# A two-layer product with four of seven partial products summed in one PSUM bank, three additions a set, and another order at the stage change

## The chip, the cores and the metric

The kernel runs on one core of one Trainium2 chip. The metric is the device time of the program in microseconds; lower is better. The engines are named as the profile names them: PE (matrix products), PEld (its weight loads), DVE (vector engine), ACT (scalar engine), POOL, and SP, whose queue issues most DMAs.

## The reference, cut to what matters

```python
scores = scale * np.matmul(q, k.transpose(0, 1, 3, 2))      # 4 batches, 12 heads, 448 x 448
scores = cap * np.tanh(scores / cap)
attn = np.exp(scores - np.max(scores, axis=-1, keepdims=True))
attn = attn / (np.sum(attn, axis=-1, keepdims=True) + 1e-09)
x = np.matmul(attn, v)                                      # laid out as 1792 tokens x 768
h = x @ w_in                                                # 768 -> 2048
g = h * np.cos(h)
out = g @ w_out                                             # 2048 -> 768
```

The weights `w_in` and `w_out` arrive as 64-bit floats and are turned into 32-bit words on the chip.

## The kernel before, in words

Three stages follow each other. **Attention** takes the first part of the program. **The first layer** multiplies `x` by `w_in`. Every factor is split into a high part and a low remainder, and each product of two factors is three matmuls (high by high, low by high, high by low). The 2 x 2 block scheme with seven products instead of eight is used: a *set* `s` is one pair of row blocks of `w_in` (index `g`, 0 to 7) with one half of the tokens (`p`, 0 or 1); there are 16 sets, listed in `ORDER`. The seven products of a set are called by the factor on the token side: `11`, `21`, `22` are blocks of `x`, `t1` to `t4` are differences of blocks. One product is 3 (pieces of the inner dimension) x 3 (high and low) = 9 matmuls of 128 x 448, so a set is 63 matmuls and the layer is 112 products. **The second layer** multiplies `g` by `w_out`, 1152 matmuls of the same size, which is 128 times nine.

A set accumulates in four PSUM banks, held as two tiles of two banks each. A tile of even sets is called `pair`, of odd sets `acc`. In `last_part` the set is brought together in SBUF: ACT copies bank a (line L797), DVE makes three additions with it (L800), then the last three products go on into banks a, d and c, ACT copies a again (L803), and DVE makes two more additions (L810). A result goes to DRAM (`hidden`) by a DMA of ACT's queue (L812). The second layer reads it back from there.

The factors of sets with p = 1 are made by DVE (`mix`, L186, a difference of blocks in place), split by ACT (`high`, L198) and by DVE (`low`, L201). For sets 2 and 3 this happens while PE works; it is the list `work[1]` and `work[2]`. Sets 0 and 1 use the p = 0 factors, which attention has made. The weights of a row block are made from raw words: ACT takes the magnitude (L257), DVE runs four steps (`clamp` L272, `shift` L275, `tail_bits` L278, `sign_bit` L282), and `sums` then makes the block sums (L306 to L312) and splits them (L544 on ACT, L293 and L299 on DVE). The words `u` have two buffers. For eight of the row blocks of `w_out` the words are stored to DRAM (`words`) and fetched again at the stage change (`fetch`), when the space of the p = 0 factors is free.

Each engine runs its instructions in the written order. What stands between the additions is taken from a list, `left`, by `fill(room)`: it takes entries until their costs (in us, written beside each) have used up the room. The second layer needs, for each `q` of 64, the gated values: ACT `turns` (L932), DVE two steps and ACT a sine (`cosine`, L937 to L939), DVE a product and ACT its high part (`gate`, L943, L944), DVE the remainder (`low`, L948); and for the first eight `q` the split of a fetched block of `w_out` (L901 on ACT, L904 on DVE). `second` issues the 18 matmuls of one `q` (L971). At the very end `evacuate` adds the last banks (L1011) and stores them (L1014).

## Time and profile before

| what | us |
|---|---|
| median of three runs | 652.08 |
| their range | 651.57 to 653.46 |
| the profiled execution's own time | 653.12 |
| its span, first to last instruction | 651.2 |
| PE busy in the span | 602.3 |
| DVE busy | 482.6 |
| ACT busy | 342.0 |

The busy time of PE is that of pipelined records, so it shows where PE stood still rather than how fast it was. DVE and ACT are busy for three quarters and half of the span. The granted clock of PE, over the whole span, is 0.971 of full speed.

### The profile page before, as it was taken

The page shows a single profiled execution, that of the slowest core. Times are in us where ns is not written, and L with a number is a line of the kernel's source. Part 1 is how long each engine was busy: PE and PEld are TensorE (multiplying, and loading weights), DVE is VectorE, ACT ScalarE, POOL GpSimd, SP SyncE. Part 2 cuts the span into 40 slices and gives each one's busy share as a digit, 9 for nine tenths or more (in the row PEclk, how much of TensorE's full clock was granted, in tenths as well). Part 3 has the DMA queues.
Part 4 walks back from the last instruction along what each step waited for, and adds up shares of the span by engine and source line. Part 5 has one row for each costly group of instructions (what it writes and reads, how often), then busy time and mean ns, then how long its engine had stood idle before and what let it go on. Part 6 is the DMA issues. An engine that isn't in the chain of part 4 may idle for free.

```text
span 651.2 us, 11970 instructions
## 1 busy us (share of the span) xinstructions
PE 602.3 (92%) x4962; PEld 467.9 (72%) x4962; DVE 482.6 (74%) x703; ACT 342.0 (53%) x479; POOL 13.0 (2%) x13
## 2 busy tenths in 40 slices
PE   9999999999837899999999788799999999999996
PEld 3333443346626799988989677699999999999985
DVE  3898999898495777777777664898796972577662
ACT  7999999991243322223222223676776662545340
POOL 0000012200000000000000000000000000000000
PEclk9999999999777999999999987899999999999999
DMA  8454334300212244364643768343333220514302
GB/s 286 141 176 128 117 120 132 110 20 2 106 56 97 106 153 153 130 199 134 233 159 125 240 225 302 106 144 123 105 109 131 85 71 0 172 69 156 115 14 88
DMA packets 39085, 83.66 MB, mean 128 GB/s; under 512 B 4339, under 2 KB 21747, under 8 KB 39027
## 3 DMA queue, kind: packets, MB, share of 16 engines
q1 hardware_dynamic: 34562, 68.86, 33.1%
q10 hardware_dynamic: 4464, 13.99, 5.3%
q8 instruction: 40, 0.66, 0.4%
q14 instruction: 19, 0.15, 0.1%
HBM read 59.51 MB, written 23.33 MB: 127 GB/s over the span
## 4 chain that ended last, share of the span: by engine, by line
PE 50%; DVE 25%; ACT 12%; DMA 8%; issue 4%; SPq 1%; ACTq 0%; DVEq 0%
PE acc L971 18%; PE pair L971 17%; DMA words<-u 5%; PE pair L409 4%; PE acc L489 4%; ACT t L428 4%; ACT t L424 4%; PE pair L730 4%; DVE sum L473 2%; PE acc L730 2%; DVE u L278 2%; DVE u L282 2%; DVE c L800 2%; ACT u L257 2%; DVE c L810 2%
## 5 line engine op out<-in xcount | busy, mean ns | idle before, releaser
L428 ACT ACTIVATE t<-t 128x1792 f32<-128x1792 f32 (+1 forms) x50 | 75.4, 1519 | 0.0
L489 PE MATMUL acc<-t,v 64*32 64x448 f32 x1344 | 73.8, 537 | 1.6 <-DVE x L527 1.5
L424 ACT ACTIVATE t<-pair 128x896 f32<-128x896 f32 x82 | 73.5, 966 | 2.9 <-PE pair L409 2.9
L409 PE MATMUL pair<-qk 64*32 64x448 f32 x1312 | 73.1, 542 | 0.3 <-ACT t L424 0.2
L489 PEld LDWEIGHTS acc<-t,v 64*32 64x32 f32 x1344 | 26.1, 107 | 39.5 <-issue 33.4
L409 PEld LDWEIGHTS pair<-qk 64*32 64x32 f32 x1312 | 25.0, 107 | 39.4 <-issue 20.7
L473 DVE TENSOR_TENSOR sum<-sum,t 128x1792 f32<-128x1792 f32 x25 | 50.5, 2019 | 0.5
L971 PE MATMUL pair<-g1h,wmixedh 128*128 128x448 f32 x96 | 30.7, 369 | 0.0
L272 DVE TENSOR_SCALAR u<-u 128x768 f32<-128x768 f32 x30 | 16.7, 556 | 16.3 <-ACT u L257 16.3
L971 PE MATMUL acc<-g1h,wmixedh 128*128 128x448 f32 x84 | 27.2, 369 | 0.0
L971 PE MATMUL acc<-g0h,wmixedh 128*128 128x448 f32 x84 | 26.6, 367 | 0.0
L939 ACT ACTIVATE f<-f 128x448 f32<-128x448 f32 x21 | 12.2, 581 | 25.8 <-DVE f L938 25.6
L939 ACT ACTIVATE f1l<-f1l 128x448 f32<-128x448 f32 x21 | 12.2, 580 | 23.9 <-DVE f1l L938 23.5
L257 ACT ACTIVATE u<-w 128x768 f32<-128x768 f32 x15 | 13.5, 900 | 21.2 <-DMA words<-u 14.7
L257 ACT ACTIVATE u<-raw 128x768 f32<-128x768 f32 x14 | 12.6, 899 | 21.7 <-DMA words<-u 13.7
L544 ACT CAST sums1h<-u 128x768 fp32r<-128x768 f32 (+1 forms) x16 | 11.7, 755 | 23.4 <-DVE u L308 13.1
L971 PE MATMUL pair<-g0h,wmixedh 128*128 128x448 f32 x72 | 23.1, 366 | 0.0
L939 ACT ACTIVATE f0l<-f0l 128x448 f32<-128x448 f32 x22 | 12.7, 579 | 17.8 <-DVE f0l L938 17.4
L971 PE MATMUL acc<-g0h,wownh 128*128 128x448 f32 x64 | 20.6, 367 | 1.4 <-ACT c L803 1.4
L971 PE MATMUL pair<-g0h,wownh 128*128 128x448 f32 x68 | 21.5, 366 | 0.0
L971 PE MATMUL pair<-g1h,wownh 128*128 128x448 f32 x52 | 17.6, 385 | 3.5 <-DVE g1h L948 2.7
L800 DVE TENSOR_TENSOR c<-c,pair 128x448 f32<-128x448 f32 x21 | 13.0, 621 | 10.0 <-ACT c L797 6.4
(405 smaller groups left out, 1628.7 us busy)
## 6 DMA issues: line engine op xcount, KB each, us to landing
hidden<-c ACTq DMA_DIRECT2D x28, 448.0 KB, 5.7
qk<-in_qk_dram SPq DMA_DIRECT2D x20, 448.0 KB, 3.9
w<-in_w_in_dram SPq DMA_DIRECT2D x18, 384.0 KB, 4.3
w<-in_w_out_dram SPq DMA_DIRECT2D x16, 384.0 KB, 3.5
raw<-in_w_out_dram SPq DMA_DIRECT2D x16, 384.0 KB, 3.6
v<-in_v_dram SPq DMA_DIRECT2D x42, 128.0 KB, 2.1
f0l<-hidden SPq DMA_DIRECT2D x22, 224.0 KB, 3.9
f<-hidden SPq DMA_DIRECT2D x21, 224.0 KB, 2.8
```

What stands on the lines that cost most here:

```text
L257: self.nc.scalar.activation(self.u[u].bitcast(F32), self.raw[k].bitcast(F32)[:, :, 1], AF.Abs, scale=F64_STEP)
L272: self.nc.vector.tensor_scalar(r, r, LEAST, MOST, op0=ALU.max, op1=ALU.min)
L278: self.nc.vector.scalar_tensor_tensor(self.u[u], self.raw[k][:, :, 0], 29, self.u[u], op0=ALU.logical_shift_right, op1=ALU.bitwise_or)
L409: self.nc.tensor.matmul(ps[o:o + 32, h, 0:S], lhsT=x[mine, k:k + 32], rhs=x[mine, Q], start=True, stop=True, tile_position=(64 * h, o))
L424: self.nc.scalar.activation(self.ts[i][:, k], self.ps.pop(j)[:, :, 0:S], AF.Tanh, scale=self.inv)
L428: self.nc.scalar.activation(t, t, AF.Exp, scale=self.capt)
L473: self.nc.vector.tensor_add(out, old, self.ts[NC * n + c])
L489: self.nc.tensor.matmul(self.acc[n, e][o, r], lhsT=self.v[n, c][rows, d], rhs=self.t(n, a, c)[rows, h], start=c == 0, stop=c == NC - 1, ti ...
L730: self.nc.tensor.matmul(out, lhsT=a, rhs=b, start=m < 4 and k == 0 and t == 0, stop=k == NQUAD - 1 and t == 2, skip_group_check=True)
L800: self.nc.vector.tensor_add(*adds[m])
L939: nc.scalar.activation(y, y, AF.Sin, scale=2.0 * math.pi)
L971: self.nc.tensor.matmul(self.out_bank(v, d)[:, 0:S], lhsT=w, rhs=x, start=v != 4 and j == 0 and i == 0, stop=v != 3 and j == HALF - 1 and ...
```

## The change: what it does

**In a set.** Four products (`11`, then `t2`, then `t3`, then `t4`) accumulate one after the other in bank 0, and after each ACT copies the running sum out (`copy1` to `copy4`); `21` has bank 3, `t1` and then `22` have bank 2. DVE makes three additions (`add1`: first sum plus bank 3; `add2`: third sum plus bank 2 when it holds `t1`; `add3`: second sum plus bank 2 when it holds both) instead of five. `step` writes these in a fixed order with the first product of the next set between, and takes the list `left` in six rooms a set; an entry can carry the step before which it isn't taken, and `until` takes entries up to a mark.

**From attention to the first layer.** The first two blocks of the second weight set are split before the words of block 3 are made, and set 1 begins with the products `11` and `21`, which need only these. The factors of p = 1 are mixed and split one after the other in the order `11`, `t1`, `21`, `t2`, `t3`, `t4`, `22` (`opening`), between the products of sets 1, 2 and 3. `t2` is now made from `t1` in its place, and `t4` from `t2`.

**From the first to the second layer.** `closing` takes the products of the last set in the order `t2`, `21`, `t3`, `t1`, `t4`, `22` after `11`, and fetches the stored words between them. The values of the second layer's q = 2, 3 and 4 get tiles of their own in the space of p = 1 factors that are done (`EARLY`), so the gating of q = 0, 1, 2 and 3 and the splits of the first three blocks stand in the last two sets. At the end of the second layer the six last banks are taken in the order 0, 2, 4, 1, 3, 5.

```diff
 ORDER = [(0, 0), (1, 0), (0, 1), (1, 1)] + [(g, p) for g in range(2, NF // 2) for p in range(2)]
 NSTEP = len(ORDER)
-PRODUCTS = (("11", 0, 0), ("t2", 5, 1), ("t3", 3, 2), ("t1", 4, 3), ("21", 1, 0), ("t4", 2, 2), ("22", 6, 3))
-ROOM = 0, 0, 0, 5.5, 3.0, 0
-ROOM_AT_ONCE = 0, 0, 0, 0, 3.0, 1.2
+PRODUCTS = {1: ("11", 0, 0, 0), 2: ("21", 1, 0, 3), 3: ("22", 6, 3, 2), 4: ("t4", 2, 2, 0),
+            5: ("t1", 4, 3, 2), 6: ("t2", 5, 1, 0), 7: ("t3", 3, 2, 0)}
+OPENING = {0: (1, 5, 6, 7)}
+ROOM = 1.6, 1.5, 1.0, 1.0, 1.2, 1.0
+ROOM_AT_END = 1.0, 1.2, 1.0, 1.2, 1.2, 1.5
 NQ = 4 * NF
 TAIL = 3
 HALF = NF // 2
 VISITS = [(t, 0) for t in range(4)] + [(t, HALF) for t in (3, 2, 1, 0)]
+EARLY = {2: "t2", 3: "11", 4: "21", 5: "22"}
...
-    def product(self, s, m):
+    def product(self, s, *ms):
 
         g, p = ORDER[s]
-        what, at, i = PRODUCTS[m]
-        out = self.bank(s, i)
...
-        self.done[s, m] = True
+        for m in ms:
+            what, at, first, i = PRODUCTS[m]
+            out = self.bank(s, i if s else first)
...
+                cols = slice(128 * k, 128 * k + 128)
+                for t, (a, b) in enumerate(terms(wh[:, cols], wl[:, cols], h[:, k], l[:, k])):
+                    self.nc.tensor.matmul(out, lhsT=a, rhs=b, start=begin and k == 0 and t == 0,
+                                          stop=k == NQUAD - 1 and t == 2, skip_group_check=True)
...
+    def end_own(self):
         nc, v = self.nc, self.nc.vector
         x = self.space.w64.bitcast(F32).rearrange("p a b -> p (a b)")
         c12, c22, c21 = [x[:, S * i:S * i + S] for i in range(3)]
         a, b, d, c = [self.bank(0, i) for i in range(4)]
-        nc.scalar.copy(c12, a)
-        v.tensor_add(c12, c12, b)
-        v.tensor_add(c22, c12, d)
-        v.tensor_add(c22, c22, c)
-        for m in (4, 5, 6):
-            self.product(0, m)
-        self.wts.words_third()
+        c11 = self.mix.tile("t4", 0, "c", [128, S], F32)
+        nc.scalar.copy(c11, a)
         v.tensor_add(c21, c12, d)
         nc.sync.dma_start(out=self.space.hidden[1][:, 0:2 * S], in_=x[:, S:3 * S])
         v.tensor_add(c12, c12, c)
         nc.sync.dma_start(out=self.space.hidden[0][:, 0:S], in_=c12)
-
...
+    def copy1(self, s):
+        self.nc.scalar.copy(self.spot(s)[0], self.bank(s, 0))
+        if s > 2:
+            self.rows[s] = self.both
+
+    def copy2(self, s):
+        self.nc.scalar.copy(self.spot(s)[1], self.bank(s, 0))
+
+    def copy3(self, s):
+        self.nc.scalar.copy(self.spot(s)[3], self.bank(s, 0))
+
+    def copy4(self, s):
+        self.nc.scalar.copy(self.spot(s)[2], self.bank(s, 0))
+        if s < 3:
+            self.store(s, 2, 3)
+        self.store_row(s, 1)
+
+    def add1(self, s):
+        c = self.spot(s)[0]
+        self.nc.vector.tensor_add(c, c, self.bank(s, 3))
+
+    def add2(self, s):
+        c = self.spot(s)[3]
+        self.nc.vector.tensor_add(c, c, self.bank(s, 2))
+
+    def add3(self, s):
+        c = self.spot(s)[1]
+        to = self.mix.x[0][:, 2] if s == 2 else c
+        self.nc.vector.tensor_add(to, c, self.bank(s, 2))
+        if s == 2:
+            self.c[s] = self.c[s][0], to, None, None
+        if s < 3:
+            self.store(s, *((1,) if s == 2 else (0, 1)))
+        self.store_row(s, 0)
+
+    def step(self, s):
+
+        self.now = s
+        if s > 3:
+            self.product(s, *((2, 5, 6) if s == 4 else (5, 6)))
+            self.fill(ROOM[0])
+            self.copy2(s)
+            if s > 4:
+                self.product(s, 2)
+            self.fill(ROOM[1])
+            self.add1(s)
+        self.product(s, 7)
+        self.fill(ROOM[2])
+        self.copy3(s)
+        self.add2(s)
+        if s % 2:
+            self.until((s // 2 + 1, 0))
+        self.product(s + 1, 1)
+        self.fill(ROOM[3])
+        self.copy1(s + 1)
+        if s == 3:
+            self.until((2, 1))
+        self.product(s, 4)
+        self.fill(ROOM[4])
+        self.copy4(s)
+        self.product(s, 3)
+        self.fill(ROOM[5])
+        self.add3(s)
+        if s % 2:
+            self.until((s // 2 + 1, 1))
+
...
+    def opening(self):
+
+        mix, v, w, act = self.mix, self.nc.vector, self.wts, self.nc.scalar
+        three = range(NQUAD)
+
+        def split(what, low=v):
+            for i in three:
+                mix.high(what, i)
+            for i in three:
+                mix.low(what, i, low)
+
+        def mixed(what):
+            for i in three:
+                mix.mix_second(i, what)
...
+        w.high(1, 5, 0, act)
+        self.product(1, 1)
+        self.copy1(1)
+        w.low(1, 3, 1, v)
+        w.low(1, 5, 0, v)
+        self.product(1, 2)
+        self.end_own()
+        self.wts.load("wi", 4)
+        split("11")
+        self.product(1, 5, 6)
+        self.copy2(1)
+        mixed("t1")
+        self.product(1, 7)
+        self.copy3(1)
+        split("t1")
+        self.product(2, 1)
+        self.copy1(2)
+        self.add1(1)
+        self.add2(1)
+        self.product(1, 4)
+        self.copy4(1)
+        split("21")
+        self.product(1, 3)
+        self.product(2, 5, 2)
+        mixed("t2")
+        split("t2")
+        self.add3(1)
+        self.add1(2)
+        self.product(2, 6)
+        self.copy2(2)
+        self.store(2, 0)
+        mixed("t3")
+        split("t3")
+        self.product(2, 7)
+        self.product(3, 1, 5, 2)
+        self.copy3(2)
+        mixed("t4")
+        split("t4")
+        self.feed()
+        self.add2(2)
+        split("22")
+        self.left.pop(0)[1]()
+        self.copy1(3)
+        self.add1(3)
+        self.product(2, 4)
+        self.fill(1.2)
+        self.copy4(2)
+        self.product(3, 6)
+        self.fill(2)
+        self.copy2(3)
+        self.product(2, 3)
+        self.add3(2)
 
...
     def fill(self, room):
-        while self.left and room > 0.3:
-            cost, call = self.left.pop(0)
+        while self.left and room > 0.3 and (len(self.left[0]) < 3 or self.left[0][2] <= self.now):
+            cost, call = self.left.pop(0)[0:2]
             call()
             room -= cost
 
...
+    def until(self, mark):
+        while mark not in self.marks:
+            self.left.pop(0)[1]()
 
...
+    def ahead(self):
+
+        t, c, g, l, h, e = self.turns, self.cosine, self.gate, self.low, self.split_high, self.split_low
+        first = (t, 0), (t, 1), (c, 0), (c, 1), (g, 0), (g, 1), (l, 0), (l, 1)
+        then = (h, 0), (t, 3), (e, 0), (c, 3), (h, 1), (t, 2), (e, 1), (g, 3), (c, 2), (l, 3), (h, 2), (g, 2), (e, 2), \
+            (t, 4), (l, 2), (c, 4), (g, 4), (l, 4)
+        cost = {t: 0, c: 1.05, g: 0.55, l: 0.55, h: 0, e: 0.88}
+        return [(cost[call], lambda call=call, q=q: call(q), NSTEP - 2 + (x is then)) for x in (first, then) for call, q in x]
...
-        work, before = self.plan()
-        for s in range(NSTEP):
+        self.left = self.plan()
+        self.now = 0
+        self.opening()
+        for s in range(3, NSTEP):
             if size is not None and s == NSTEP // 2:
                 bits = self.nc.values_load(size.bitcast(I32))
-            self.left += work[s]
-            if s == NSTEP - 1:
+            if s == NSTEP - 2:
                 self.get(0)
                 self.get(1)
-                self.left += self.ahead(0)
...
-        self.last_part(NSTEP - 1, (0, 0, 0, 99, 0, 0))
+                self.left += self.ahead()
+            if s == NSTEP - 1:
+                self.closing(s)
+            else:
+                self.step(s)
...
             elif j == HALF - 1:
-                for d in range(6):
+                for d in (0, 2, 4, 1, 3, 5):
                     for k in range(TAIL):
                         self.second(q - TAIL + 1 + k, d)
                     self.evacuate(v, d // 2, d % 2)
```

The order of instructions at three places. First DVE, at the start of the p = 1 factors (`x_129` to `x_131` are the three pieces of `x`; `s...l` are low remainders; lines L186 and L191 are mixing, L201 and L206 a remainder). Before:

```order
L201 TENSOR_TENSOR s22l<-x_129,s22h 128x448
L201 TENSOR_TENSOR s22l<-x_130,s22h 128x448
L201 TENSOR_TENSOR s22l<-x_131,s22h 128x448
L186 TENSOR_TENSOR x_129<-x_129 128x448
L186 TENSOR_TENSOR x_130<-x_130 128x448
L186 TENSOR_TENSOR x_131<-x_131 128x448
L201 TENSOR_TENSOR s21l<-x_129,s21h 128x448
L186 TENSOR_TENSOR x_129<-x_129 128x448
L201 TENSOR_TENSOR st2l<-x_129,st2h 128x448
L201 TENSOR_TENSOR st3l<-x_129,st3h 128x448
L201 TENSOR_TENSOR st1l<-x_129,st1h 128x448
L201 TENSOR_TENSOR st4l<-x_129,st4h 128x448
```

After:

```order
L191 TENSOR_TENSOR x_129<-x_129 128x448
L191 TENSOR_TENSOR x_130<-x_130 128x448
L191 TENSOR_TENSOR x_131<-x_131 128x448
L206 TENSOR_TENSOR st1l<-x_129,st1h 128x448
L206 TENSOR_TENSOR st1l<-x_130,st1h 128x448
L206 TENSOR_TENSOR st1l<-x_131,st1h 128x448
L835 TENSOR_TENSOR c22h<-c22h,acc 128x448
L839 TENSOR_TENSOR c22l<-c22l,acc 128x448
L206 TENSOR_TENSOR s21l<-x_129,s21h 128x448
L206 TENSOR_TENSOR s21l<-x_130,s21h 128x448
L206 TENSOR_TENSOR s21l<-x_131,s21h 128x448
L191 TENSOR_TENSOR x_129<-x_129 128x448
```

Before, all pieces of several differences were mixed ahead of the first remainder of `t2`; now each factor is mixed, split and followed by the additions of set 1 (`c22h`, `c22l` are the results of set 1).

Second ACT, in sets 4 to 6 of the steady part (`c...` are results of a set, `hidden` the DMAs that store them, `sums...` and `own` weight blocks; L257 and L266 are the magnitude). Before:

```order
L797 COPY c_2665<-pair 128x448
L544 CAST sums1h<-u_87 128x384
L544 CAST sums1h<-u_86 128x768
L544 CAST sums1h<-u_87 128x768
L544 CAST sums1h<-u_86 128x768
L803 COPY c_2665<-pair 128x448
L257 ACTIVATE u_87<-w_85 128x768
L812 DMA hidden_95<-c_2665 128x896
L812 DMA hidden_94<-c_2665 128x896
L797 COPY c_2760<-acc 128x448
L257 ACTIVATE u_86<-raw 128x768
```

After:

```order
L817 COPY c_2658<-acc 128x448
L828 COPY c_2551<-pair 128x448
L813 DMA hidden_95<-c_2551 128x896
L553 CAST sums_2229<-u_87 128x768
L813 DMA hidden_94<-c_2551 128x896
L553 CAST sums_2229<-u_86 128x768
L822 COPY c_2658<-acc 128x448
L266 ACTIVATE u_87<-w_85 128x768
L825 COPY c_2658<-acc 128x448
L266 ACTIVATE u_86<-raw 128x768
L817 COPY c_2752<-pair 128x448
L828 COPY c_2658<-acc 128x448
```

Two copies a set have become four (L817, L822, L825, L828), and the magnitudes and casts stand between them.

Third DVE, in the last two sets (`f...` and `g...` are values of the second layer, `wownl` a fetched weight block). Before:

```order
L810 TENSOR_TENSOR c_3503<-c_3503,acc 128x448 x2
L800 TENSOR_TENSOR c_3604<-c_3604,pair 128x448 x3
L937 TENSOR_SCALAR f0l<-f0l 128x448
L938 TENSOR_TENSOR f0l<-f0l 128x448
L937 TENSOR_SCALAR f0l<-f0l 128x448
L938 TENSOR_TENSOR f0l<-f0l 128x448
L943 TENSOR_TENSOR f0l<-f0l 128x448 x2
L948 TENSOR_TENSOR g0h<-f0l,g0h 128x448 x2
L810 TENSOR_TENSOR c_3604<-c_3604,pair 128x448 x2
L800 TENSOR_TENSOR c_3669<-c_3669,acc 128x448 x3
L904 TENSOR_TENSOR wownl<-wownl,wownh 128x768
L937 TENSOR_SCALAR f_3661<-f_3661 128x448
```

After:

```order
L1128 TENSOR_TENSOR f0l<-f0l 128x448 x2
L1133 TENSOR_TENSOR g0h<-f0l,g0h 128x448 x2
L835 TENSOR_TENSOR c_3590<-c_3590,acc 128x448
L1077 TENSOR_TENSOR wownl<-wownl,wownh 128x768
L1122 TENSOR_SCALAR f11h<-f11h 128x448
L1123 TENSOR_TENSOR f11h<-f11h 128x448
L839 TENSOR_TENSOR c_3590<-c_3590,acc 128x448
L1077 TENSOR_TENSOR wownl<-wownl,wownh 128x768
L1128 TENSOR_TENSOR f11h<-f11h 128x448
L1122 TENSOR_SCALAR ft2h<-ft2h 128x448
L1123 TENSOR_TENSOR ft2h<-ft2h 128x448
L1133 TENSOR_TENSOR g11l<-f11h,g11l 128x448
```

Before, the last set's additions stood among the values of q = 0, 1 and 2; now they stand among those of q = 0 to 3 (`f11h` is q = 3, `ft2h` q = 2).

## Rows read from the trace of the kernel before

**Rows 1.** The page: PE's busy tenths and its granted clock in 40 slices.

```profile
PE   9999999999837899999999788799999999999996
...
PEclk9999999999777999999999987899999999999999
```

**Rows 2.** Stages: length, busy us (instructions) of PE, PEld, DVE, ACT, POOL; clock; DMA.

```profile
156.32:181.69 25.37, 21.86 (x90) 18.61 (x91) 15.25 (x26) 5.80 (x10) 0.00 (x0) 0.87 0.19 68
181.69:204.87 23.18, 9.19 (x28) 6.58 (x27) 20.50 (x36) 10.22 (x20) 0.00 (x0) 0.63 0.12 43
204.87:363.67 158.80, 153.38 (x740) 138.26 (x738) 115.37 (x171) 42.55 (x63) 0.00 (x0) 1.00 0.48 159
363.67:424.35 60.68, 47.67 (x199) 41.82 (x198) 39.02 (x62) 23.64 (x38) 0.00 (x0) 0.89 0.65 222
424.35:633.73 209.38, 209.38 (x1024) 192.36 (x1023) 152.96 (x281) 118.53 (x206) 0.00 (x0) 1.00 0.31 99
```

**Rows 3.** PE in time, 156 to 204 us: start, length, instruction [idle before, releaser].

```profile
156.32 0.47 PE L730 MATMUL pair<-ownh,sums0h 128*128 128x448 f32 x1 [0.36 <-DVE w L749]
...
164.77 0.47 PE L730 MATMUL acc<-ownh,sums1l 128*128 128x448 f32 x1 [1.80 <-DVE sums1l L293]
...
167.88 0.74 PE L730 MATMUL acc<-mixedh,sums1h 128*128 128x448 f32 x1 [1.03 <-ACT sums1h L544]
...
197.42 0.74 PE L730 MATMUL pair<-st2h,sums0h 128*128 128x448 f32 x1 [6.37 <-ACT st2h L198]
```

**Rows 4.** PE in time, 306 to 418 us.

```profile
306.33 0.47 PE L730 MATMUL pair<-mixedh,sums1h 128*128 128x448 f32 x1 [1.40 <-DVE c L810]
...
373.16 0.47 PE L730 MATMUL acc<-s11h,sums1h 128*128 128x448 f32 x1 [3.75 <-ACT c L803]
...
375.17 0.58 PE L730 MATMUL acc<-s11l,sums1h 128*128 128x448 f32 x1
375.54 0.58 PE L730 MATMUL acc<-st2h,sums1h 128*128 128x448 f32 x1
...
392.22 0.74 PE L730 MATMUL acc<-s21h,sums1h 128*128 128x448 f32 x1 [4.34 <-DVE c L800]
...
417.62 0.67 PE L971 MATMUL pair<-g1h,wownh 128*128 128x448 f32 x2 [2.75 <-DVE g1h L948]
```

**Rows 5.** PE and DVE in time, from 635 us to the end.

```profile
635.23 0.47 PE L971 MATMUL pair<-g0h,w22h 128*128 128x448 f32 x1 [0.71 <-DVE ot1h L1011]
...
646.30 0.37 PE L971 MATMUL pair<-g1h,wt3h 128*128 128x448 f32 x1
```

**Rows 6.** DVE groups in the steady part: count, busy us, mean ns of one.

```profile
L800 DVE TENSOR_TENSOR c<-c,pair 128x448 f32<-128x448 f32 x15 | 9.3, 621 | 5.7 <-ACT c L797 5.3
L293 DVE TENSOR_TENSOR sums1l<-u,sums1h 128x768 fp32r<-128x768 f32 x9 | 8.3, 954 | 2.9 <-ACT sums1h L544 2.9
```

**Rows 7.** DVE and ACT in time: last word step, a copy, casts, remainders, mixing.

```profile
160.41 0.56 DVE L329 SCALAR_TENSOR_TENSOR u<-third,u 128x384 int32<-128x384 int32 x1
...
178.24 0.53 ACT L803 COPY ct4h<-acc 128x448 f32<-128x448 f32 x1 [5.44 <-PE acc L730]
178.67 1.50 ACT L198 CAST s11h<-x 128x448 fp32r<-128x448 f32 x3
...
185.23 1.69 DVE L201 TENSOR_TENSOR s22l<-x,s22h 128x448 fp32r<-128x448 f32 x3
186.84 1.69 DVE L186 TENSOR_TENSOR x<-x 128x448 f32<-128x448 f32 x3
```

**Rows 8.** ACT's waits, 204 to 424 us: in total, times, longest.

```profile
ACT u L257 <- DMA words<-u: 28.3, 6, 5.0
```

**Rows 9.** ACT group of the steady part, and DMA issues with us to landing.

```profile
L257 ACT ACTIVATE u<-w 128x768 f32<-128x768 f32 x7 | 6.3, 900 | 13.8 <-DMA words<-u 9.9 <-issue 3.0 <-DVE sums1l L293 0.9
...
words<-u SPq DMA_DIRECT2D x8, 384.0 KB, 7.0
wownl<-words SPq DMA_DIRECT2D x5, 384.0 KB, 4.2
```

More of the change, by code (lines that the diff above doesn't have):

```diff
@@ L758, in end @@
         nc.sync.dma_start(out=self.space.hidden[0][:, 0:S], in_=c12)
[L760 to L776 removed]
+        nc.scalar.dma_start(out=self.space.hidden[0][:, S:2 * S], in_=c11)
@@ new lines, in spot @@
+    def spot(self, s):
+        if s not in self.c:
+            x = self.mix.x
+            if s == 1:
+                one, two = [self.mix.tile("22", part, "c", [128, 2, S], F32) for part in range(2)]
+                self.c[s] = one[:, 1], one[:, 0], two[:, 1], two[:, 0]
+            elif s == 2:
+                u = [u.bitcast(F32)[:, 0:S] for u in self.space.u]
+                self.c[s] = u[0], u[1], x[0][:, 1], x[0][:, 0]
+            else:
+                x = x[1] if s == 3 else self.mix.four(s % 2, "c")
+                self.c[s] = x[:, 1], x[:, 0], x[:, 3], x[:, 2]
+                self.both = x[:, 0:2], x[:, 2:4]
+        return self.c[s]
@@ new lines, in closing @@
+    def closing(self, s):
+        self.now = s
+        self.get(3)
+        self.fetch(0)
+        self.fetch(1)
+        self.product(s, 6)
+        self.get(2)
+        self.fetch(2)
+        self.fill(ROOM_AT_END[0])
+        self.copy2(s)
+        self.product(s, 2)
+        self.get(4)
+        for f in range(3, HALF):
+            self.fetch(f)
+        self.fill(ROOM_AT_END[1])
+        self.add1(s)
+        self.product(s, 7)
+        self.fill(ROOM_AT_END[2])
+        self.copy3(s)
+        self.product(s, 5)
+        self.fill(ROOM_AT_END[3])
+        self.add2(s)
+        self.product(s, 4)
+        self.fill(ROOM_AT_END[4])
+        self.copy4(s)
+        self.product(s, 3)
+        self.fill(ROOM_AT_END[5])
+        self.add3(s)
+        self.fill(99)
@@ L869, in plan @@
[L869 to L872 removed]
         mag = self.magnitude
[L874 to L875 removed]
+        own, last = self.sums(2)[0:3], self.sums(2)[3:]
```

241 lines of the change are left out of this document (105 added, 136 removed).

## The prediction

> **What bounds the kernel now.** I read the page's slices first: PE is nearly full except in two dips, and the clock falls in the same slices [rows 1]. Next came a table of stages cut at these dips [rows 2], then PE in order of time inside them, for what ended each wait [rows 3, 4], and last the prices of what DVE and ACT do there [rows 6 to 9].
>
> The measure is PE's pace when nothing stops it. From 424.35 to 633.73 us PE is busy without a gap at full clock: 209.38 us for 1023 matmuls (1024 are counted, one of which began earlier) [rows 2], 0.205 us each. A product of nine takes 1.845 us. At 156.32 us, where the attention's work on PE is over [rows 3], 3 products of set 0, 105 of the other sets and 1152 / 9 = 128 such groups of the second layer are left: 236 x 1.845 = 435.4 us. The last matmul would start 0.2 us before 156.3 + 435.4 = 591.7, at 591.5. Before, it starts at 646.30 [rows 5] and the span ends at 651.2, 4.9 us later. With that end the span would be 596.4, so PE loses 54.8 us.
>
> Where: 156.32 to 181.69 holds 10 products (18.45 us), loss 6.9; to 204.87 it holds 3 (5.5), loss 17.6; to 363.67 it holds 82 (151.3), loss 7.5; to 424.35 it holds 22 (40.6), loss 20.1 [rows 2]; behind 633.73, 48 matmuls (9.8 us) take 646.5 - 633.7 = 12.8, loss 2.9 [rows 5]. That is the whole sum but for rounding. In the second stretch PE waits for factors: 6.37 us at once for a cast of `t2` [rows 3], with DVE busy 20.5 of 23.2 us [rows 2]. In the fourth it waits 3.75 for a copy, 4.34 for an addition, 2.75 for a gated remainder [rows 4]. After such waits a matmul comes only every 0.37 us (375.17 to 375.54), the mean clock of that stretch being 0.89, and 0.63 in the second [rows 2, 4]. DVE is busy 115.4 of 158.8 us in the steady part [rows 2], so it has slack; only the order holds PE up there, 1.40 us before the second product of a set in one period [rows 4].
>
> **The change, part by part.** I take the losses that remain in the new order, with these prices: addition 0.65 (621 ns and a gap), split of a weight block 0.95 [rows 6]; three remainders or three mixings 1.6, three casts 1.5, a copy 0.53 [rows 7], a magnitude 0.90 [rows 9]. A matmul's record is 0.37 long against its 0.205 of pace, so a reader of its bank starts 0.16 after PE could go on.
>
> *Attention to set 1.* The words of block 3 end on DVE at 160.97 (160.41 + 0.56) [rows 7]; the split written ahead of them puts that at 161.95. PE no longer cares: it runs set 0's last three products, then `11` and `21` of set 1, from 156.3 to 165.6. Meanwhile DVE makes one remainder and four block sums, to 165.5, and the split for `t1`, to 166.5. PE waits 0.7 for it. Before, waits of 1.80 and 1.03 and half a clock stood here [rows 3].
>
> *Opening.* Mixing and splitting cost what they cost before: 12 mixings, 21 casts and 21 remainders; on DVE 33 x 0.54 = 18 us. They are now laid among the products of sets 1 to 3, 14 products or 26 us of PE. Followed step by step, with each engine in its written order: `t2` and `t3` of set 1 stand next to each other in bank 0, so copy2 is bare, 0.16 + 0.53 and two hand-overs, loss 0.95; the casts of `t1` wait in ACT behind copy3, DVE stands 2 us, `22` of set 1 waits for add2, loss 0.5; the casts and remainders of `t3` end at 187.7 where PE wants them from 184.4, loss 1.75; `11` of set 4 needs its weight block, made after add3 of set 2, loss 1.15. All else is ready in time. Sets 0 to 2, five products of set 3 and one of set 4 are then done at 203.8. The next weights arrive just too late for `t1` of set 4 (0.7), and at `t3` of set 4 copy2 stands in ACT behind a store that waits for add3 of set 3 and behind a magnitude (0.90), so PE waits 2.95. The sum to there: 0.7 + 0.95 + 0.5 + 1.75 + 1.15 + 0.7 + 2.95 = 8.7 us. 32 products stand ahead of `t3` of set 4, 28 of them after 156.3, so it starts at 156.3 + 28 x 1.845 + 8.7 = 216.7.
>
> *Clock.* Waits of 3 us and more were followed by half clock here (3.75 at 373.16, slow by 375.17 [rows 4]); 1.40 alone was not (the stretch around it has 1.00 [rows 2, 4]); 1.80 and 1.03 close together were (0.74 long at 167.88 [rows 3]). Of my waits one is of the first kind. Ten matmuls at 0.37 in place of 0.205 cost 1.7; I take 2.0, with bounds 0 and 5.
>
> *Steady part.* Five additions become three and two copies four: DVE gives back 2 x 0.65 a set, ACT takes 2 x 0.53 more of the 7 x 1.845 = 12.9 us of a set, where it is busy 42.6 of 158.8 [rows 2]. Neither is the path. What matters is that each of copy1 to copy3 has one product of another bank (1.845) between its reading and the next writing of bank 0: it needs 0.16 + 0.53 + 0.1 = 0.8, so 1.0 is spare. The entry that can eat this is the magnitude that waits for a store of words: 4.7 us each, six times, in ACT [rows 8], landing 7.0 after issue [rows 9]. It now stands behind copy4 and ahead of the row's store, where the next copy is 4 us off. Hidden; if that cover went, 4.7 - 4 and up to 4.7 a period. I take 0.5 for the whole part, bounds 0 and 10.
>
> Against the edit speaks this: if no product of another bank covers a copy, PE stands 0.8 at each of copy1 to copy3, in 13 sets (3 to 15) 13 x 3 x 0.8 = 31 us. By the rows the copy (0.53 [rows 7]) is shorter than the product between, so I count none of it here and make it rival 4. [...]
>
> *Stage change.* The last set's `11` is taken one step ahead, the gates of q = 0 to 3 run beside sets 14 and 15, and every product of set 15 but the last pair has another bank to go on with. I follow DVE: words 5 to 7, four pairs of steps of the gates, three splits and six additions, some 27 us against 13 products, 24 us; what does not fit is needed only for q = 2 and later, 7 us after. The fetches start when set 14 is done and land 4.2 later [rows 9], while PE has 11 us of products. The tightest point is the remainders of q = 5 to 7, where DVE comes 0.2 to 0.6 late: 1.0 in all, bounds 0 and 8 (eight fetches of 384 KB one behind another).
>
> *Tail.* Banks in the order 0, 2, 4, 1, 3, 5 put a product of another tile between an addition and the next writing of its tile; three waits of 0.71 [rows 5] with what each costs in the pipeline go, 2.9 us.
>
> **Sum.** Losses after: 8.7 + 2.0 + 0.5 + 1.0 = 12.2 in place of 54.8: 42.6 us less. The profiled execution took 653.12, its span 651.2 and 1.9 around it: 610.5 after. The median of the runs is 1.04 below the profiled one, 652.08 - 42.6 = 609.5.
>
> **The rivals.**
> 1. *Copies reach PE.* A magnitude or a cast in ACT stands in front of copy2 or copy3 in most sets and uses up the spare 1.0: about 0.8 more in each of 13 sets, 10 us, 620. For it: ACT's order is fixed and it has waits of up to 5.0 [rows 8]. Against: those waits don't stand there.
> 2. *Stage change stays long.* DMAs or DVE hold up q = 1 to 4, and the clock falls once more: 6 to 8 us, 617.
> 3. *The opening hardly shrinks.* ACT and DVE hand each factor over in turns, so a 0.5 us slip at each of seven factors comes on top, and the clock stays at half through it (0.63 now [rows 2]): 12 us more, 622.
> 4. *One bank serializes; at its worst, slower than before.* Every copy of bank 0 is bare: 31 us (above), 609.5 + 31 = 640. It decides against the kernel before when a copy costs PE 42.6 / 39 = 1.09 or more, which one store wait in front of it brings: with the six waits' 28.3 [rows 8] on top it is 669. For it: each copy has a spare of 1.0 only, and the waits stand on the same engine. Against: the product between, and the written order, which has those waits behind copy4.
> 5. *The change doesn't do what it says:* the waits for factors only move from set 2 to set 3 with the same length, and the stage change too; then 650 to 654.
>
> **How the numbers follow.** What a measurement of this kernel can tell from no change is about 0.3%, 2 us. Forecast (604 to 614): 0.62. Rival 1: 0.13. Rival 2: 0.12. Rival 3: 0.08. Rival 4: 0.035, of which 0.025 slower than before. Rival 5: 0.015. The range holds most of the forecast's and rival 2's cases and half of rival 1's: 603 to 620. Its lower end is the forecast without the clock's 2.0 and with 4 of the 8.7 away, the lowest that PE's pace allows being 597. Faster 0.96, same 0.015, slower 0.025.
>
> **What would show it.** PE's first wait above 1 us should stand near 184 to 188 (`t3` of set 2) and the largest, near 3, at `t3` of set 4 about 214 to 217; the second layer should begin near 367; from set 5 to 14 PE should have no waits over 0.5; at the stage change none over 1; the clock 1.00 but for one or two short spells. Wrong would be: copies of bank 0 as releasers of PE in every set (rival 1), fetched words or gated remainders as its releasers (rival 2), casts of factors with several us (rival 3).

## The result and the profile after

The changed kernel takes 609.75 us (median of four runs, 606.88 to 610.45) against 652.77 for the kernel before, a ratio of 0.9332 (95% interval 0.9297 to 0.9368). The forecast was 609.5. The profiled execution took 610.45 with a span of 608.6, where the working had 610.5 and 608.6. That the sum came out to the microsecond is partly luck: the clock cost more than its term, other terms and PE's pace less, as shown below.

The page of the changed kernel: busy shares, and PE and its clock in 40 slices, to be set against [rows 1].

```profile
span 608.6 us, 11953 instructions
...
PE 591.2 (97%) x4962; PEld 463.2 (76%) x4962; DVE 463.2 (76%) x673; ACT 357.9 (59%) x509; POOL 13.0 (2%) x13
...
PE   9999999999998989999999999999999999999996
...
PEclk9999999999998979999999999999999999999999
```

Of the two dips one small one is left, in the slices 13 to 15 (about 183 to 228 us). The second, at the stage change, is gone, and so is the notch at the end but for the stores behind the last matmul.

Stages of the changed kernel, cut at its own places: length, then busy us (instructions) of PE, PEld, DVE, ACT, POOL; clock; DMA.

```profile
156.37:181.69 25.32, 24.13 (x115) 21.28 (x116) 20.23 (x35) 10.43 (x20) 0.00 (x0) 1.00 0.24 87
181.69:225.00 43.31, 37.98 (x158) 32.72 (x157) 33.97 (x55) 17.70 (x31) 0.00 (x0) 0.88 0.42 144
225.00:368.63 143.63, 143.53 (x703) 131.40 (x702) 100.24 (x149) 56.61 (x90) 0.00 (x0) 1.00 0.56 190
368.63:390.00 21.37, 21.37 (x106) 19.47 (x105) 16.24 (x28) 13.76 (x23) 0.00 (x0) 1.00 0.71 266
390.00:591.00 201.00, 201.00 (x988) 185.22 (x987) 152.85 (x281) 117.57 (x204) 0.00 (x0) 1.00 0.31 103
```

Against [rows 2]: from 156.37 to 181.69 PE now has 115 matmuls recorded in place of 90, at full clock in place of 0.87. From 225.00 to 390.00 it is busy but for 0.1 us. DVE there works 116.5 of 165.0 us (100.24 + 16.24), ACT 70.4. Nearly all that is lost lies between 181.69 and 225.

PE of the changed kernel in order of time: every wait over 0.3 us from 157 us to the end, and the first and the last matmul of the second layer.

```profile
166.32 0.47 PE L745 MATMUL acc<-mixedh,sums 128*128 128x448 f32 x1 [0.37 <-DVE sums L302]
170.66 0.68 PE L745 MATMUL acc<-mixedh,sums 128*128 128x448 f32 x2 [0.62 <-ACT c22h L822]
...
185.66 0.47 PE L745 MATMUL pair<-st3h,sums0h 128*128 128x448 f32 x1 [1.33 <-ACT st3h L203]
...
186.67 0.54 PE L745 MATMUL pair<-st3l,sums0h 128*128 128x448 f32 x1 [0.33 <-DVE st3l L206]
...
203.92 0.47 PE L745 MATMUL pair<-ownh,sums0l 128*128 128x448 f32 x1 [0.52 <-DVE sums0l L302]
...
211.88 0.47 PE L745 MATMUL pair<-mixedh,sums0l 128*128 128x448 f32 x1 [0.36 <-DVE sums0l L302]
...
218.29 0.74 PE L745 MATMUL pair<-mixedh,sums0h 128*128 128x448 f32 x1 [2.68 <-ACT c L822]
...
368.83 0.36 PE L1156 MATMUL pair<-g0h,wownh 128*128 128x448 f32 x1
...
603.59 0.37 PE L1156 MATMUL pair<-g,wt3h 128*128 128x448 f32 x1
```

The names say which product waits: `mixedh,sums` at 166.32 is `t1` of set 1, at 170.66 its `t3` behind copy2 (L822); `st3h` is `t3` of set 2; `ownh,sums0l` is `11` of set 4, and `mixedh` on `pair` its `t1` and `t3`. In [rows 3, 4] single waits were 6.37, 4.34 and 3.75; the largest is now 2.68. The second layer begins at 368.83, in the kernel before at 400.63. In the product of `t3` of set 2 and again behind 218.29 matmuls come every 0.37 us for a while in place of 0.205. The granted clock reads 0.54 from 186.67 to 190.36 and 0.50 from 218.29 to 224.43; such a stretch is called half clock below.

### The profile page after: what moved, and what is told of

Read it like the earlier page. It is cut to its first block, busy times and chain, and to the rows that moved or that the text cites. A ratio compares the mean times of both kernels' runs of the same rounds, so it can differ in the third digit from the quotient of the medians.

```text
span 608.6 us, 11953 instructions
## 1 busy us (share of the span) xinstructions
PE 591.2 (97%) x4962; PEld 463.2 (76%) x4962; DVE 463.2 (76%) x673; ACT 357.9 (59%) x509; POOL 13.0 (2%) x13
## 4 chain that ended last, share of the span: by engine, by line
PE 74%; DVE 12%; ACT 10%; issue 2%; DMA 1%; ACTq 0%; SPq 0%; DVEq 0%
PE pair L1156 19%; PE acc L1156 19%; PE acc L745 15%; PE pair L745 11%; PE pair L418 5%; PE acc L498 4%; ACT t L437 4%; ACT t L433 4%; DVE sum L482 3%; DVE x L536 1%; DMA raw<-in_w_out_dram 1%; DVE u L287 1%; ACT u L266 1%; PE idle L67 1%; DVE u L284 1%
## 5 line engine op out<-in xcount | busy, mean ns | idle before, releaser
L1124 ACT ACTIVATE f<-f 128x448 f32<-128x448 f32 x38 | 22.1, 581 | 46.6 <-DVE f L1123 46.1
L281 DVE TENSOR_SCALAR u<-u 128x768 f32<-128x768 f32 x30 | 16.7, 557 | 12.9 <-ACT u L266 12.1
L1117 ACT ACTIVATE f<-f,angles 128x448 f32<-128x448 f32 x38 | 25.4, 667 | 1.3 <-DMA f<-hidden 1.3
L1123 DVE TENSOR_TENSOR f<-f 128x448 f32<-128x448 f32 x38 | 23.8, 626 | 1.3
L1122 DVE TENSOR_SCALAR f<-f 128x448 f32<-128x448 f32 x38 | 14.8, 390 | 11.9 <-ACT f L1117 11.8
L1128 DVE TENSOR_TENSOR f<-f 128x448 f32<-128x448 f32 x38 | 23.5, 619 | 0.0
L745 PE MATMUL pair<-mixedh,sums0h 128*128 128x448 f32 x48 | 18.4, 384 | 2.8 <-ACT c L822 2.7
L745 PE MATMUL pair<-mixedh,sums0l 128*128 128x448 f32 x48 | 18.4, 383 | 1.7 <-DVE sums0l L302 1.7
L284 DVE TENSOR_SCALAR u<-u 128x768 int32<-128x768 int32 x32 | 17.9, 560 | 1.1
L745 PE MATMUL pair<-mixedl,sums0h 128*128 128x448 f32 x48 | 18.1, 378 | 0.0
```

The costliest lines, as they stand in the source:

```text
L284: self.nc.vector.tensor_single_scalar(self.u[u], self.u[u], 3, op=ALU.logical_shift_left)
L745: self.nc.tensor.matmul(out, lhsT=a, rhs=b, start=begin and k == 0 and t == 0, stop=k == NQUAD - 1 and t == 2, skip_group_check=True)
L1117: self.nc.scalar.activation(v, h, AF.Identity, bias=self.quarter, scale=1.0 / (2.0 * math.pi))
L1123: nc.vector.tensor_sub(y, v, y)
L1124: nc.scalar.activation(y, y, AF.Sin, scale=2.0 * math.pi)
L1128: self.nc.vector.tensor_mul(y, h, y)
```

## The experiments

All are edits of the changed kernel. Beside each median (of four runs, five for the control and the two kernels with more than one fix) stands the ratio to the kernel before, run on the same chip, with its interval. The changed kernel itself, run again as a control, gave 609.58 us (0.9326, 0.9303 to 0.9348); differences below are taken to that. The runs with both fixes, with five additions and with the later gates stood on the control's chip, the others on a second one, where the kernel before was 0.5 to 0.7 us faster. By the ratios the differences come out up to 1 us otherwise and keep their signs (4.1 in place of 5.0 for set 4, 2.8 in place of 3.5 for `t3`, 1.5 in place of 0.8 for the tail). As runs of the changed kernel spread over 3.6 us, four of them don't tell a difference of about 1 us from nothing.

**Control.** 

> The changed kernel once more, unedited, beside the others of this group. Both theories: 607 to 611; the waits of PE the same to 0.05 us, while the stretches of half clock behind them need not come back at the same places, since its four runs so far had clocks of 0.990 to 0.997.

Its profiled span is 605.5 us; the waits of PE are those above to 0.02 us (1.33 at `t3` of set 2, 2.69 at `t3` of set 4), but for 0.18 in place of 0.37 at `t1` of set 1. But the clock is 1.00 behind the wait at `t3` of set 2, where it had been half. So executions of one kernel differ by how often the clock falls; the waits don't differ. In what follows a theory is judged by waits and their releasers first, and by medians second.

**A bare copy in every set.** `21` stands ahead of `t2`:

```diff
-            self.product(s, *((2, 5, 6) if s == 4 else (5, 6)))
+            self.product(s, *((2, 5, 6) if s == 4 else (5, 2, 6)))
...
-            if s > 4:
-                self.product(s, 2)
```

> In sets 5 to 14 `21` is taken ahead of `t2`, so `t2` and `t3` stand next to each other in bank 0 and copy2 has no product of another bank beside it; nothing else moves. My theory (the product between hides the copy; a bare one costs PE its 0.16 + 0.53 and a hand-over): 10 sets x 0.8 = 8 us more than the 609.8 of the changed kernel, 617 to 618.5, with copy2 as PE's releaser in each of the ten sets, idle 0.6 each. Rival a (PE doesn't need the cover, the copy overlaps anyhow): 609 to 611 and no such waits. Rival b (ACT's order makes a bare copy as dear as in set 4, 2.7 idle): 10 x 2.8 = 28 us more, about 638, with a clock that falls in many sets.

615.9 us (0.9423, 0.9397 to 0.945), 6.3 more than the control, and below the 617 to 618.5 that were forecast. PE in order of time: the first and the last of ten equal rows.

```profile
233.22 0.47 PE L745 MATMUL acc<-st3h,sums0h 128*128 128x448 f32 x1 [0.62 <-ACT c L822]
...
357.02 0.67 PE L745 MATMUL pair<-mixedh,sums 128*128 128x448 f32 x2 [0.62 <-ACT c L822]
```

Nine sets take 123.80 us between them, 13.76 each, where 63 matmuls at 0.205 are 12.9: a bare copy costs 0.85, ten of them 8.5, as my theory has it (0.8 each). The profiled spans differ by 9.9 (615.4 against 605.5), that and a longer stretch of half clock in set 4 (16 matmuls against 10); the medians show 6.3. In the kernel as changed no such row exists in these sets, so the one product of another bank between hides the copy wholly. Rival b fell: where ACT stands idle ahead of the copy, a bare copy is cheap, and the clock stayed at 1.00 through these ten waits.

**The wait at set 4.** The third addition of set 3 goes ahead of its room's entry, copy2 of set 4 ahead of the magnitude:

```diff
         self.product(s, 3)
+        if s == 3:
+            self.add3(s)
         self.fill(ROOM[5])
-        self.add3(s)
+        if s > 3:
+            self.add3(s)
...
+            if s == 4:
+                self.copy2(s)
             self.fill(ROOM[0])
-            self.copy2(s)
+            if s > 4:
+                self.copy2(s)
```

ACT of the changed kernel ahead of the wait: the store of set 3's rows (2.62 us for its two issues, while DVE's L844 is awaited), the magnitude (L266), then copy2 (L822).

```profile
213.65 0.52 ACT L828 COPY x<-acc 128x448 f32<-128x448 f32 x1
214.20 2.62 ACTq L813 DMA_DIRECT2D hidden<-x  x2
216.92 0.89 ACT L266 ACTIVATE u<-raw 128x768 f32<-128x768 f32 x1 [2.75 <-DVE x L844]
217.71 0.52 ACT L822 COPY c<-pair 128x448 f32<-128x448 f32 x1
```

> In set 3 the third addition goes ahead of the entry that fills its room, and in set 4 copy2 ahead of the magnitude. My theory (the wait of 2.68 at `t3` of set 4 is ACT's order: a store that waits for this addition, then a magnitude of 0.9, then copy2): the wait falls to 0.7 to 1.1, and the half clock behind it (about 17 matmuls at 0.37) goes if a wait of 1 us alone doesn't bring it: 1.7 to 4.8 us less than 609.8, so 605 to 608. Rival (the wait is the weights' or the bare copy itself): the wait stays at 2.5 or more and the time at 609 to 611.

604.54 us (0.9264, 0.9228 to 0.9301), 5.0 less, just below the forecast range. The wait at this place is now 0.85, and the clock behind it 1.00 in the profiled run. That is 0.23 more than the 0.62 of the bare copies above, for copy2 still stands behind the issues of the store:

```profile
211.94 1.62 ACTq L813 DMA_DIRECT2D hidden<-x  x2
213.61 0.53 ACT L822 COPY c<-pair 128x448 f32<-128x448 f32 x1 [1.70 <-PE pair L745]
```

So the 1.8 us that went were the written order, and not the weights or the bank: the magnitude in ACT, and in DVE a step of the words that had stood ahead of the addition which the store awaits. The run moves both at once and doesn't price them apart. These 1.8 us of waiting bring more than their length, because half clock went with them (16 matmuls, 2.9 us, in the changed kernel's profile).

**`t3` of set 2 one product later.**

```diff
-        self.product(2, 7)
-        self.product(3, 1, 5, 2)
+        self.product(3, 1)
+        self.product(2, 7)
+        self.product(3, 5, 2)
```

> On PE `11` of set 3 is taken ahead of `t3` of set 2. My theory (the factor `t3` is 1.5 us late and any product that has its factors can cover it): the waits of 1.33 and 0.33 at `t3` go, and the half clock behind them too: 2 to 4 us less than 609.8, 606 to 608. Rival (ACT and DVE hand the lateness on: copy3 of set 2 comes 1.85 later and pushes the casts of `t4` and `22` behind it): the same 1.5 to 2 us stands at the next factors or at `11` of set 4, 609 to 611.

606.11 us (0.9283, 0.9253 to 0.9312), 3.5 less. No wait over 0.3 stands between 171 and 199 us, and the later ones in the first layer are as before (0.53, 0.35, 2.70): the lateness is covered and not handed on.

**Both.** 

> The edits of set 4 and of `t3` of set 2 together. My theory (separate links, and PE alone sets the pace between them): the waits of 1.33 and 0.33 gone and the one of 2.7 at 0.9, so 3.8 us of waits less, and no half clock after 157 us in most runs: a span near 601, 602 to 604. Rival (the 1.5 us saved at set 2 only make the weights of set 4 late): waits for weights at `11` and `t1` of set 4 grow by 1 to 1.5, 604 to 607.

602.55 us (0.9216, 0.9198 to 0.9234), all five runs within 602.01 and 602.64. This beats both kernels: 7.0 us below the changed one, 50.9 below the kernel before. Its stage of the opening, to be set against the second row of the stages above:

```profile
181.69:225.00 43.31, 41.43 (x197) 36.42 (x196) 37.52 (x60) 20.92 (x36) 0.00 (x0) 1.00 0.49 166
```

197 matmuls recorded in place of 158, at full clock. The waits left after 157 us are 0.62, 0.53, 0.34 and 0.85.

**One place further.** On top of both, the cast of the first blocks of set 4 goes ahead of a store that waits for an addition:

```diff
         self.product(2, 3)
+        self.left.pop(0)[1]()
         self.add3(2)
```

> The two edits of the kernel with both fixes, and in the opening the cast of the first two weight blocks of set 4 one place earlier in ACT's order, ahead of the store that waits for the third addition of set 2. My theory (that cast stands in ACT behind the store, though its words are ready 2 us before): the waits of 0.53 and 0.25 at `11` of set 4 go; of the 1.04 they cost, 0.3 to 0.5 come back at `t1` of set 4, whose blocks hang on a copy behind PE: 0.5 to 0.8 less than 602.55, about 601.9. Rival (the blocks hang on PE's last product of set 2 and not on ACT's order): 602 to 603, with the same wait.

602.54 us (0.9221, 0.9199 to 0.9243): nothing. The wait at `11` of set 4 went as forecast, but it came back in full, and a little more, at `t1` of set 4. PE there, and the copy in ACT that is behind it:

```profile
207.31 0.48 PE L745 MATMUL pair<-mixedh,sums0h 128*128 128x448 f32 x1 [0.94 <-ACT sums0h L553]
...
208.50 0.47 PE L745 MATMUL pair<-mixedh,sums0l 128*128 128x448 f32 x1 [0.72 <-DVE sums0l L302]
```

```profile
197.85 0.33 ACTq L806 DMA_DIRECT2D hidden<-x  x1
...
203.66 0.53 ACT L817 COPY c<-pair 128x448 f32<-128x448 f32 x1 [3.29 <-DMA hidden<-x]
204.09 0.52 ACT L553 CAST sums0h<-u 128x384 fp32r<-128x384 f32 x1
```

copy1 of set 4 waits for the store issued at 197.85, which reads the space that copy1 writes, and the cast stands behind copy1. My theory named the copy but held PE for its releaser; it is a transfer. PE is early enough here to meet the next bound. That bound is there in the kernel with both fixes too, where copy1 waits for the same store until 202.85; here the store, issued at the same time, landed 0.8 later, which is the little more.

**Is DVE the path at `t3`?** Three maxima of a piece with itself ahead of the mixing of `t3`, which leave the data as they are:

```diff
         self.store(2, 0)
+        for i in three:
+            x = mix.x[i][:, 2]
+            v.tensor_max(x, x, x)
         mixed("t3")
```

> Ahead of the mixing of `t3` DVE makes three maxima of a piece with itself (128 x 448, nothing changes): 1.6 us more on DVE in the opening. My theory (at `t3` of set 2 PE hangs on DVE): the wait of 1.33 becomes 2.9 and nothing takes it up later but a part of the wait for weights at `11` of set 4: 1.0 to 1.6 more of waits, and half clock behind it in most runs, 611 to 614. Rival (ACT's casts and copies bound it, with DVE standing 1.2 to 2.2 at three places): less than 0.5 more.

610.39 us (0.9337, 0.9308 to 0.9367), 0.8 more. The wait at `t3` is 2.94, so 1.61 longer, the three operations to the tenth, and the remainder's 0.33 behind it is gone. So DVE's time counts one for one here. The median shows half of it, which four runs don't tell from nothing, and stays below the forecast of 611 to 614.

**The split of `21` ahead of `t1`.**

```diff
         split("11")
+        split("21")
...
         self.copy4(1)
-        split("21")
```

> The factor `21` is split right behind `11`, ahead of `t1`, in the stretch in which DVE stands 2.2 us. My theory (DVE's order bounds the opening at `t3`, and 1.9 of its waits come from handing over with ACT): `t1` keeps its time, everything from `t2` on comes 2 to 3 us earlier, the waits of 1.33 and 0.33 at `t3` go; copy2 of set 1 stands behind three more casts, 0.5 more there: 1 to 1.5 us less and less half clock, 606 to 608.5. Rival (ACT bounds the opening): `t1` comes 1.5 later for its three casts, `22` of set 1 and `t1` of set 2 wait as much, 610 to 612.

607.13 us (0.9291, 0.9258 to 0.9324), 2.5 less and in the forecast range, but not by the forecast way. The first mixing for `t2` begins at 176.29 in place of 180.11, 3.8 earlier; the wait at `t3` fell only from 1.33 + 0.33 to 1.09. DVE and ACT of this run at that place:

```profile
182.28 0.62 DVE L835 TENSOR_TENSOR u<-u,pair 128x448 f32<-128x448 f32 x1 [1.78 <-PE pair L745]
182.81 1.69 DVE L191 TENSOR_TENSOR x<-x 128x448 f32<-128x448 f32 x3
```

```profile
184.13 0.53 ACT L822 COPY u<-pair 128x448 f32<-128x448 f32 x1 [4.96 <-PE pair L745]
...
184.56 1.50 ACT L203 CAST st3h<-x 128x448 fp32r<-128x448 f32 x3
```

DVE's first addition of set 2 and ACT's copy2 stand ahead of the mixing and the casts of `t3`, and both wait for PE itself. So in the changed kernel two chains arrive at `t3` almost together: the factors of DVE, and the written order behind PE's own last product. Taking time from the first alone leaves 1.09. copy2 of set 1 waits 0.90 in place of 0.62, so the waits of PE over 0.3 come to 5.88 in place of 6.21: most of the 2.5 is not waiting. The clock behind the 1.09 was 1.00 in the profiled run; where the rest comes from stays open.

**Set 1 without its head start.** `21` is taken after `t2`, as a cover of copy2:

```diff
         self.product(1, 1)
...
-        self.product(1, 2)
         self.end_own()
...
         self.copy2(1)
+        self.product(1, 2)
```

> In set 1 `21` is taken after `t2` and no longer ahead of `t1`; DVE's and ACT's orders are as in the changed kernel. My theory (`21` fills the time in which the blocks for `t1` are made): the wait at `t1` of set 1 grows from 0.36 to 2.2, while `21` now covers copy2, whose 0.62 goes: 1.1 more, and half clock in most runs, 610 to 613. Rival (the blocks are not late, the 0.36 is a hand-over): 608.5 to 609.5, by the covered copy.

607.61 us (0.9295, 0.9263 to 0.9328), 2.0 *less*, against the forecast of 610 to 613. The waits are as my theory has them:

```profile
165.52 0.47 PE L745 MATMUL acc<-mixedh,sums 128*128 128x448 f32 x1 [1.37 <-ACT sums L553]
166.52 0.47 PE L745 MATMUL acc<-mixedh,sums 128*128 128x448 f32 x1 [0.52 <-DVE sums L302]
```

1.89 in place of 0.37, and no wait for copy2; with the pipeline 2.34 against 0.51 + 0.77, 1.06 more. The time went the other way. In the profiled run the clock is half behind this early wait (the matmuls from 167.06 to 170.41), but 1.00 behind the waits of 1.34 and 2.70 that come later; the four spans are 604.1 to 607.2, those of nine runs of the changed kernel 605.1 to 608.6. So the head start is worth 1 us of waiting, and whether an early wait makes a later fall of the clock rarer stays open; four runs don't settle it.

**Five additions again.**

```diff
         self.nc.vector.tensor_add(c, c, self.bank(s, 3))
+        if s > 3:
+            self.nc.vector.tensor_max(c, c, c)
```

and the same behind the second addition.

> Behind the first and the second addition of sets 4 to 15 DVE makes a maximum of the sum with itself (128 x 448, the result unchanged), so DVE has five instructions of that size a set again: 24 x 0.6 = 14 us more work. My theory (DVE had slack in the steady part, the number of additions isn't the path there): 0 to 1.5 us more than the changed kernel, and that in set 4 or the last set. Rival (fewer additions are what made the steady part free of waits): up to 14 us more, with additions or casts of weights as PE's releasers in every set.

610.17 us (0.9346, 0.9319 to 0.9373), 0.6 more, within the spread, for 15 us of work on DVE (24 maxima of 0.625). The only new waits of PE stand at 353.13 (0.84, for the second addition of set 14, which the maxima hold up) and 359.32 (0.38, for copy2), where the gates are laid in the same sets. So the smaller number of additions is not what freed the steady part.

**The gates one set later.**

```diff
-            if s == NSTEP - 2:
+            if s == NSTEP - 1:
                 self.get(0)
```

> The fetch of q = 0 and 1 and the list of gates and splits start one set later, with set 15 in place of set 14. My theory (the early start carries the stage change: two gates are 4.3 us of DVE that then stand in the last set, which is full): waits at q = 0 to 4 on gated remainders or splits of 3 to 6 us in all, and half clock once: 612 to 617. Rival (the order of the products of the last set alone is what removed the waits): no more than 1 us of waits, 609 to 611.

614.01 us (0.9407, 0.938 to 0.9435), 4.4 more: the size of my theory, by another mechanism. PE's longest wait, and ACT and SP ahead of it:

```profile
360.51 0.66 PE L745 MATMUL acc<-st3h,sums 128*128 128x448 f32 x2 [2.91 <-ACT c L822]
```

```profile
357.67 1.24 ACT L1117 ACTIVATE f0l<-f0l,angles 128x448 f32<-128x448 f32 x2 [5.03 <-DMA f0l<-hidden]
...
359.94 0.51 ACT L822 COPY c<-acc 128x448 f32<-128x448 f32 x1
```

```profile
344.81 8.07 SPq L1016 DMA_DIRECT2D words<-u  x2
352.98 1.33 SPq L1113 DMA_DIRECT2D f0l<-hidden  x2
```

The fetch of q = 0 and 1 is issued at 352.98, behind stores that hold SP's queue; ACT waits 5.03 for it with copy2 of set 15 behind, and PE waits for copy2. Two waits of 0.48 and 1.75 for a weight split and a gated remainder follow at 379.75 and 389.40, the second with half clock behind it. What the early start buys is first of all the landing of a transfer, and only then DVE's time. It is also what rival 4 described, a transfer in ACT's order ahead of a bank 0 copy, and it costs 2.9 where it happens.

**The tail in the order 0 to 5.**

```diff
-                for d in (0, 2, 4, 1, 3, 5):
+                for d in range(6):
                     for k in range(TAIL):
```

> The last six banks are taken in the order 0 to 5 again. My theory (in that order a bank's addition holds the tile that the next bank's products want): three waits of 0.7 come back and cost with the pipeline 2.9 us, 612.7. Rival (the tail's waits went because the additions come earlier in the changed kernel, not by the order): no waits, 609 to 611.

610.39 us (0.9349, 0.9317 to 0.938), 0.8 more. The three waits are back, each 0.71, the first of them:

```profile
592.62 0.47 PE L1156 MATMUL pair<-g0h,w22h 128*128 128x448 f32 x1 [0.71 <-DVE ot1h L1196]
```

Each puts the matmul behind it 0.87 later than the pace and the one after that 0.1 later again: from 591.54 to 603.68 45 matmuls take 12.1 us in place of 9.2, so the loss is the 2.9 forecast, and the order is the cause. The median shows 0.8 of it and lies in the rival's range; this profiled run had one stretch of half clock where the changed kernel's had two, so the median alone would have misled.

## Why the prediction was right, and where it was not

**The measure.** PE's pace set the end. The last matmul starts at 603.59, 12.1 us behind the 591.5 that 236 products of nine would allow; forecast 12.2. The end of the span is 5.0 behind it, forecast 4.9.

**Opening, term by term.** Each with what its place cost beyond the pace: `t1` of set 1 0.7, measured 0.52; copy2 of set 1 0.95, measured 0.77; `22` of set 1 0.5, measured 0.36; `t3` of set 2 1.75, measured 1.98; `11` of set 4 1.15, measured 1.04; `t1` of set 4 0.7, measured 0.52; `t3` of set 4 2.95, measured 2.84. Sum 8.7, measured 8.0 for the waits alone. Behind each wait the next matmul also comes 0.1 late; from 156.37 to 218.29, 61.9 us for 28 products of 1.845, 10.3 are lost, 8.7 without the 1.6 of half clock at `t3` of set 2. So the sum is that of the forecast. The longest stood at 218.29, forecast 216.7. Following each engine in its written order, with durations from the trace, gave every place and every releaser. Two experiments removed the two largest terms and showed their causes to be those of the working; for `t3` of set 2 the working named only the casts and remainders, and the run with `21` first showed copy2 and an addition behind PE as a second chain of the same length.

**Clock: mis-sized.** The term was 2.0, for one fall of ten matmuls, the author's estimate, behind the wait of 2.95. The profiled execution had two: from 186.67 to 190.36 (1.6 us) and from 218.29 to 224.43 (2.9 us), so 4.5, near the bound of 5. The control had the second alone. The rule drawn from [rows 3, 4], that only 3 us and more or two waits close together are followed by half clock, did not hold: the 1.33 and 0.33 here are such a pair, and were followed by it in two executions out of eight. The kernel before had already spoken against it. Its 2.75 at 417.62 [rows 4] was followed by a clock of 0.64, and the close pair below by 1.00; the prediction took up neither:

```profile
223.92 0.47 PE L730 MATMUL pair<-mixedh,sums0h 128*128 128x448 f32 x1 [1.25 <-ACT sums0h L544]
224.91 0.48 PE L730 MATMUL pair<-mixedh,sums0l 128*128 128x448 f32 x1 [0.52 <-DVE sums0l L293]
```

```profile
417.70:422.00 4.30, 4.30 (x15) 3.87 (x16) 3.83 (x6) 3.32 (x7) 0.00 (x0) 0.64 0.28 68
225.50:229.00 3.50, 3.50 (x19) 3.25 (x18) 3.29 (x7) 1.16 (x2) 0.00 (x0) 1.00 0.00 0
```

**Steady part and stage change: mis-sized the other way.** 0.5 and 1.0 were allowed; neither lost anything, with no wait of PE over 0.3 from 219 us to the end: the 80 products from 218.29 to 368.83 take 150.5 us, 147.6 of pace and the 2.9 of half clock. This takes back 1.5 of the 2.5 that the clock cost beyond its term. The rest is the pace: from 368.83 to 603.59 PE takes 234.8 us for 1151 matmuls, 0.204 each, where 0.205 gives 236.0. So 8.7 + 4.5 - 1.2 = 12.0, and the sum held by terms that happened to cancel. The store waits that were to be hidden behind copy4 (28.3 in [rows 8]) are not in the list of ACT's waits at all: the stores of words now land in 2.7 us in the median, before 7.0 [rows 9]. At the stage change the fetches landed later than the 4.2 forecast, and PE had enough products to cover it. The DMA issues of the changed kernel, with us to landing at the end:

```profile
words<-u SPq DMA_DIRECT2D x8, 384.0 KB, 2.7
wownl<-words SPq DMA_DIRECT2D x5, 384.0 KB, 6.0
```

**Tail.** 2.9 forecast, 2.9 by the run with the old order.

**Rivals.** Rival 1 (copies reach PE in most sets) and rival 4 (one bank serializes) need a bare copy; with the product between, no copy released PE from set 5 to set 15 in the changed kernel. Where the product between is taken away a copy costs 0.85, and one product of another bank of 1.845 is cover enough here, as long as the copy is not late for another reason. In the run for set 4 copy3 of the last set was:

```profile
356.96 0.83 ACT L1080 CAST wownh<-wownl 128x768 fp32r<-128x768 f32 x1 [3.01 <-DMA wownl<-words]
```

```profile
358.83 0.67 PE L745 MATMUL acc<-st4h,own 128*128 128x448 f32 x2 [0.71 <-ACT c L825]
```

The cast waited for fetched words with copy3 behind it, and PE waited 0.71. In the changed kernel the same cast waits 1.39 and PE not at all, so the stage change has little to spare. Rival 3 did not come, and rival 2 in earnest only when the gates were put back by a set. Rival 5 is out by the stages.

## What to carry to other kernels

Where one engine is the bound, give it a pace per unit of work, turn every stretch into a loss against it, and walk each other engine's written order; a wait is then a place in an order, and moving one instruction there can be worth more than removing work (two reorderings gave 7 us, while two extra vector operations a set cost 0.6, within the spread). A copy out of a shared bank was free here as long as one product elsewhere covered it (no wait of PE over 0.3 from 219 us on), and dear when a transfer (2.91, the later gates) or a store's wait (2.68, set 4) stood ahead of it in its engine's order. Judge edits of this size by the waits of the trace as well as by the median, because the clock fell in some executions and not in others: a loss of 2.9 in the tail showed as 0.8 in the median, and 3.5 of waits removed as 7.0.
